# The second scoring of a tile's last 64 columns reads Q's high part from the first transposed block

## The chip, the cores and the metric

The kernel runs on one core of a Trainium2 chip. The metric is device time in microseconds (us), the median of the runs shown. Engines are named as the profile names them: PE is TensorE (PEld its weight loads), DVE is VectorE, ACT is ScalarE, POOL is GpSimd, SP is the queue that issues most DMAs.

## The reference

Attention over 8 batches x 8 heads, 576 rows of 64 numbers each, where every row keeps only its 32 largest scores; its output goes through a mixture of 8 experts, each of which takes 576 rows.

```
scores = q @ k.T / 8
kth = 32nd largest score of each row
scores = where(scores >= kth, scores, -1e9)
attn = softmax(scores);  x = attn @ v          # [4608, 512]
logits = x @ w_gate                            # greedy: the largest logits first, 576 rows an expert
out[rows of e] = relu(x[rows of e] @ w1[e]) @ w2[e]
```

## The kernel before, in words

**Pairs and tiles.** Attention goes over 32 pairs of heads, the experts follow. A pair has 9 tiles of 128 query rows (tiles 0 to 3 of one head, 5 to 8 of the other, tile 4 the last 64 rows of both, in two halves of 64 partitions).

**High and low parts.** Q and K are scaled and split into a high and a low f16 part, and turned by transposing DMAs (L394, for the first pair L395). Q's turned tile Qt has two blocks. The first, Q1, holds Q's high part on partitions 0 to 63 and its low part on 64 to 127. The second, Q2, holds the high part again on partitions 0 to 63, and on partition 64 a number per query row, 0 at first. K2 holds K's high part twice, K3 K's low part on partitions 0 to 63 and a constant on partition 64. KZ (two buffers, L251 to L252 and L396) holds K's low part of the last 128 columns on partitions 0 to 63, and zeros on 64 to 127.

**The work of a tile** (`tile_ops`, L429). PE scores it (L444 to L449): Q1 with K2 plus Q2 with K3, 512 columns ("s0") and the last 64 ("s1"). DVE takes the 8 largest of each of six chunks of 96 columns (L453, L454) and from these 48 the 24 largest in order (L457 to L461). ACT marks the scores above the 24th (`sign`, L466). PE then pushes the marked scores far down: `move(1)` for 512 columns ("o0", L471), `move(0)` for the last 64 ("o1"), which scores these 64 columns a second time (L470: Q1 with K2 plus Q2 with KZ), then adds the marks (L471) and eight more columns (L472). DVE finds the next 8 (`next8`, L473), so the 32nd is known; ACT makes a second mask from it (`relu`, L479). The scores stand in four PSUM lanes; a lane is free after L479.

**The row maxima.** As soon as the largest scores of three tiles (a trio) are known, POOL puts them beside Q's high part (`most`, L500), and one transposing DMA on SP writes these three tiles of Q2 anew, now with the maxima on partition 64 (`q2`, L501; three a pair, 96 in all, one for each trio). Q2 is thus written twice for a tile: by L394, and by L501.

**Softmax and values.** For each tile PE makes the turned masks (L515) and the scores turned (L520 with Q1, L521 with rows 0 to 64 of Q2, so with the maxima subtracted); ACT takes the exponential (L525), POOL splits it into two f16 parts (L528, L531), PE multiplies by V (L622), ACT scales (L596).

**What sets the order.** Every engine's order of work is fixed when the program is built: each step has a due time from a table (TAU, L268, period 24.5 us a pair) and a planner (`Loom`, L144) merges them. The planner's edges know that L501 needs the maxima and that the masks of a trio come after it; they hold nothing between L501 and `move(0)`. The semaphores come afterwards from the tile framework: it looks at what each instruction reads and writes, in the order of the plan. Where L501 stands in the plan between two `move(0)` of its trio, it waits for the reads of Q2 before it, and the reads of Q2 after it wait for its landing. SP's queue is in order; it also carries the loads of Q, K and V and L394.

Of the kernel before, what the change touches and what calls it, by code (L numbers as in the profile page):

```python
# [210 lines left out]
def attention(tc, q,k,v,w_gate,x_out,L,acc,cuts, pairs,ahead=()):  # L211
# [3 lines left out]
    with ExitStack() as ctx:  # L215
# [9 lines left out]
        def part(slot,kind,x,e):  # L225

            j,a=slot%(LANES//2),slot//(LANES//2)
            tc.add_to_no_dep_group(f"{j}{a}{kind}{e}",x.ins)
            for g in {"o":(f"{j}{1-a}o",f"{j}{1-a}m",f"{j}{1-a}t",f"{j}{a}t"),"t":(f"{j}{1-a}o",f"{j}{a}o"),"m":(f"{j}{1-a}o",)}[kind]:
                for o in "VAP":  # L230
                    if o!=e: tc.declare_no_dep(x.ins,group=g+o,reason="another bank")
            return x
# [15 lines left out]
        for i in range(2):  # L248
            t=cp.tile([128,2,9,128],F16,name=f"nq{i}"); NQ.append(t); V.memset(t[:,1,:,64:128],0.0)
            t=cp.tile([128,2,9,128],F16,name=f"nk{i}"); NK.append(t); V.memset(t[:,1,:,65:128],0.0); V.memset(t[:,1,:,64:65],-QS)  # L250
        KZ=[cp.tile([128,128],F16,name=f"kz{i}") for i in range(2)]  # L251
# [6 lines left out]
        def rims():  # L258
# [19 lines left out]
            k0=[15.592283,19.276599,21.411347,23.340401,28.448154,29.061625,31.74815,36.460414,37.611696],   # L278
# [150 lines left out]
        def tile_ops(P,i):  # L429
# [5 lines left out]
            def at_(): return D["at"]["slot"]  # L435
            def side(): return at_()//(LANES//2)
            def span(a,b):

                s_ps=SS[at_()%(LANES//2)]; o=960*side()
                return s_ps[:,o+a:o+b]  # L440
# [4 lines left out]
            def products(Q,K,n_,o,k0,kind,first,last):  # L445
                for h in ([0] if i<4 else ([1] if i>4 else [0,1])):
                    if i==4: rows=slice(h*64,h*64+64); qc=slice(512+h*64,576+h*64)
                    else: rows=slice(0,128); qc=slice(i*128,i*128+128)
                    part(at_(),kind,T.matmul(o[rows],P[Q][:n_,qc],P[K][:n_,k0(h):k0(h)+o.shape[1]],start=first,stop=last,skip_group_check=True),"P")  # L449
# [17 lines left out]
            def move(half):  # L467
                u=side(); o=64*u if half else 512*(1-u); n_=512 if half else 64
                if not half:
                    for Q,K,k0 in (("Q1","K2",512),("Q2","KZ",0)): products(Q,K,128,span(o,o+64),lambda h: k0+64*h,"t",Q=="Q1",False)  # L470
                part(at_(),"o" if half else "t",T.matmul(span(o,o+n_),off,P["w"][i][:,o:o+n_],start=False,stop=bool(half),skip_group_check=True),"P")  # L471
                if not half: part(at_(),"t",T.matmul(span(-8,0) if u else span(576,584),off,D["fw"][:,0:2,0:4],start=False,stop=True,skip_group_check=True),"P")  # L472
            def next8(): part(at_(),"m",V.max(P["st"][:,i,24:32],span(-8,576) if side() else span(0,584)),"V")  # L473
# [15 lines left out]
            p=tw=go("sg",sign,[p],take="w",e="A",d=0.717); mid.append(p)  # L489
            f_=go("fl",fill,[p],e="V",d=.11)  # L490
            p=go("o0",lambda: move(1),[p],e="P",d=.218)
            p=go("o1",lambda: move(0),[p,f_,P["kz"]],e="P",d=.125 if i==4 else .093,m=i==4); mid.append(p)
            p=go("y8",next8,[p],e="V",d=0.69); mid.append(p)
            p=go("rl",relu,[p],take="r",free=[ts],e="A",d=.63); P["tr"][i]=[p,tw]; mid.append(p)
# [925 lines left out]
```

## Time and profile before

| what | value |
|---|---|
| median of 3 runs | 1504.88 us (1500.55 to 1507.64) |
| profiled execution | 1496.38 us |
| its span, first to last instruction | 1494.7 us |
| attention, from the profile's lines | about 15 to 1040 us |
| mean granted clock of PE | 0.945 of 2.4 GHz |

The profile's page shows one execution: busy time of each engine, then groups of instructions with what they waited for. "Idle before" is the time the engine stood still ahead of an instruction, with the instruction or DMA that ended the wait. Matmuls overlap, and the shown length of one is longer than the distance to the next, so a busy PE is not PE at its peak. Granted clock is a share of 2.4 GHz: 0.50 means 1.2 GHz.

### The profile page before, as it was taken

The numbers are of one execution on the slowest core, as the hardware profiler recorded it, in microseconds if no ns is written. First come the engines' busy times: TensorE is split into PE (matmuls) and PEld (weight loads), VectorE is DVE, ScalarE is ACT, GpSimd is POOL, SyncE is SP. The second block draws the span as 40 slices with busy tenths as digits, with TensorE's granted clock in tenths as the row PEclk, the third lists the DMA queues.
The fourth block names the chain that finished last, engine by engine and source line by source line (L and its number), as shares of the span: only waits on it lengthen the run. The fifth ranks groups of instructions, "written<-read, shape, count | busy, mean of one in ns | idle before, by whom it ended". The sixth has DMA issues, their size and how long they took to land. (4 is left out here: it accounts for less than half of the span.)

```text
span 1494.7 us, 45618 instructions
## 1 busy us (share of the span) xinstructions
PE 1280.0 (86%) x17276; PEld 954.3 (64%) x17277; DVE 1102.4 (74%) x5557; ACT 934.4 (63%) x2177; POOL 822.2 (55%) x1090
## 2 busy tenths in 40 slices
PE   7778887888887888887888787888698999999998
PEld 5666666666666666666666665667674666566654
DVE  7777787877867777786777777786698999885410
ACT  3777777877867777786777777786133444325411
POOL 3776777767767776776676776775112312221011
PEclk9999999999989999998899999899699999999999
DMA  5443354334335343444433434330246666667001
GB/s 110 81 80 69 68 113 91 74 73 102 77 62 130 65 84 66 99 88 84 98 66 83 100 74 89 84 83 11 96 140 173 178 198 201 205 182 213 26 33 34
DMA packets 313130, 148.97 MB, mean 100 GB/s; under 512 B 278532, under 2 KB 294916, under 8 KB 311876
## 3 DMA queue, kind: packets, MB, share of 16 engines
q1 hardware_dynamic: 306530, 126.53, 36.1%
q0 software_dynamic: 5968, 19.14, 4.1%
q8 instruction: 137, 2.24, 0.6%
q14 instruction: 93, 0.76, 0.2%
q10 hardware_dynamic: 402, 0.29, 0.1%
HBM read 71.60 MB, written 18.87 MB: 61 GB/s over the span
## 5 line engine op out<-in xcount | busy, mean ns | idle before, releaser
L453 DVE MAX8 cd<-s 128x8 f32<-128x96 f32 x1440 | 318.2, 250 | 23.5 <-PE s L449 22.8
L449 PEld LDWEIGHTS <-Qt 128*128 128x128 f16 (+1 forms) x1920 | 149.7, 105 | 264.6 <-DMA Qt<-nq 189.2
L473 DVE MAX8 st<-s 128x8 f32<-128x584 f32 x288 | 216.8, 762 | 117.3 <-PE s L472 100.8
L449 PE MATMUL s<-Kt,Qt 128*128 128x64 f16 (+3 forms) x1600 | 289.5, 282 | 11.2 <-ACT w L466 8.1
L479 ACT ACTIVATE r<-s,st 128x576 bf16<-128x576 f32 x288 | 210.5, 739 | 130.9 <-DVE st L473 120.2
L531 POOL TENSOR_TENSOR elm<-F,ehm 128x512 f16<-128x512 f32 x253 | 287.8, 1159 | 0.2
L466 ACT ACTIVATE w<-s,st 128x576 uint16<-128x576 f32 x288 | 214.1, 743 | 60.9 <-PE s L472 50.8
L528 POOL TENSOR_SCALAR ehm<-F 128x512 f16<-128x512 f32 x253 | 154.4, 619 | 144.6 <-ACT F L525 144.3
L449 PE MATMUL s<-kz,Qt 128*128 128x64 f16 (+1 forms) x320 | 58.2, 206 | 169.3 <-DMA Qt<-nq 169.3
L1269 PE MATMUL ph<-xT,w1h 128*128 128x288 f16 (+1 forms) x1024 | 190.3, 286 | 3.6 <-DMA xT<-xs 3.6
L521 PE MATMUL pt<-Qt,Kt 65*128 65x128 f16 (+1 forms) x1280 | 179.4, 219 | 0.3 <-DMA Qt<-nq 0.3
L520 PE MATMUL pt<-Qt,Kt 128*128 128x128 f16 (+1 forms) x1280 | 179.2, 218 | 0.0
L525 ACT ACTIVATE F<-pt 128x512 f32<-128x512 f32 x256 | 148.8, 594 | 43.4 <-PE pt L521 39.9
L1329 POOL DMA_INDIRECT out_dram<-ob,idx x39 | 42.1, 1079 | 239.0 <-ACT ob L1324 222.4
L471 PE MATMUL s<-w,off 128*128 128x512 f16 (+1 forms) x576 | 154.0, 299 | 0.3 <-ACT w L466 0.2
L1269 PE MATMUL ph<-xT,w1l 128*128 128x288 f16 (+1 forms) x512 | 146.1, 286 | 0.0
L454 DVE MAX8 cd<-s 128x8 f32<-128x96 f32 x288 | 73.3, 255 | 90.0 <-PE s L449 58.2
L622 PE MATMUL pv<-vh,ehm 128*128 128x65 f16 x1012 | 124.2, 199 | 1.4 <-DVE xb L640 0.4
L622 PE MATMUL pv<-vh,elm 128*128 128x65 f16 x1012 | 124.4, 198 | 0.0
L622 PE MATMUL pv<-vl,ehm 128*128 128x65 f16 x1012 | 124.4, 198 | 0.0
L520 PEld LDWEIGHTS <-Kt 128*128 128x128 f16 x1280 | 120.7, 101 | 4.4 <-issue 0.7
L521 PEld LDWEIGHTS <-Kt 65*128 65x128 f16 x1280 | 120.5, 100 | 4.1 <-issue 0.3
(314 smaller groups left out, 3635.3 us busy)
## 6 DMA issues: line engine op xcount, KB each, us to landing
wr<-in_moe_w_dram SPq DMA_DIRECT2D x32, 1024.0 KB
kn<-in_k_dram SPq DMA_DIRECT2D x32, 256.0 KB
vt<-in_v_dram SPq DMA_DIRECT2D x64, 128.0 KB
x<-xb SPq DMA_DIRECT2D x8, 1024.0 KB
qn<-in_q_dram SPq DMA_DIRECT2D x31, 256.0 KB
Qt<-nq SPq DMA_TRANSPOSE x129
kn<-in_k_dram SPq DMA_DIRECT2D x32, 32.0 KB
vt<-in_v_dram SPq DMA_DIRECT2D x64, 16.0 KB
```

Source lines behind the costliest of these rows:

```text
L449: part(at_(),kind,T.matmul(o[rows],P[Q][:n_,qc],P[K][:n_,k0(h):k0(h)+o.shape[1]],start=first,stop=last,skip_group_check=True),"P")
L453: if c<5: part(at_(),"o",V.max(o,main(512-CW-CW*c,512-CW*c) if u else main(CW*c,CW*c+CW)),"V")
L466: part(at_(),"m",A.activation(D["w"],span(0,576),AF.Sign,bias=P["st"][:,i,32:33],scale=(1+2.0**-21),accum_out=acc[:,col]),"A")
L471: part(at_(),"o" if half else "t",T.matmul(span(o,o+n_),off,P["w"][i][:,o:o+n_],start=False,stop=bool(half),skip_group_check=True),"P")
L473: def next8(): part(at_(),"m",V.max(P["st"][:,i,24:32],span(-8,576) if side() else span(0,584)),"V")
L479: part(at_(),"m",A.activation(r,span(0,576),AF.Relu,bias=P["st"][:,i,31:32],scale=-1.0),"A")
L520: T.matmul(o,K2[:,kb:kb+128],Q1[:,qc],start=False,stop=False,skip_group_check=True)
L521: T.matmul(o,K3[0:65,kb:kb+128],Q2[0:65,qc],start=False,stop=(c==3 and h==sub[-1][0]),skip_group_check=True)
L528: G.tensor_scalar(D["eh"],D["E"],1.0,0.0,op0=ALU.mult,op1=ALU.add)
L531: G.tensor_tensor(el,D["E"],D["eh"],op=ALU.subtract); P["e"][i]=(D["eh"],el)
L622: for m_ in (range(N-3) if part==0 else range(N-3,N)): T.matmul(out,seq[m_][0],seq[m_][1],start=(m_==0),stop=(m_==N-1))
L1269: P.matmul(B["ph"][:,lo-c0:hi-c0],a[:,c,fs],xT[:,b+c,lo:hi],start=(i==0),stop=(i==11),skip_group_check=True)
```

## The change

The second product of the second scoring reads Q1 in place of Q2. Partitions 64 to 127 of KZ are zero, so the low part of Q in Q1 meets zeros, as partition 64 of Q2 did. The mark of the first product (it starts the sum) is taken from K's name, since Q's name is now the same for both. Nothing else is changed.

```
             def move(half):
                 u=side(); o=64*u if half else 512*(1-u); n_=512 if half else 64
                 if not half:
-                    for Q,K,k0 in (("Q1","K2",512),("Q2","KZ",0)): products(Q,K,128,span(o,o+64),lambda h: k0+64*h,"t",Q=="Q1",False)
+                    for Q,K,k0 in (("Q1","K2",512),("Q1","KZ",0)): products(Q,K,128,span(o,o+64),lambda h: k0+64*h,"t",K=="K2",False)
                 part(at_(),"o" if half else "t",T.matmul(span(o,o+n_),off,P["w"][i][:,o:o+n_],start=False,stop=bool(half),skip_group_check=True),"P")
```

## Rows read from the trace of the kernel before

**Rows 1.** Windows: us, busy time (instructions) of each engine, granted clock, DMA share, GB/s

```profile
100.00:1035.00 935.00, 772.55 (x12586) 608.47 (x12587) 717.08 (x4173) 707.60 (x1744) 670.56 (x902) 0.93 0.38 82
1035.00:1495.00 460.00, 433.07 (x3510) 285.47 (x3508) 311.55 (x933) 165.61 (x292) 94.07 (x92) 0.96 0.45 137
```

**Rows 2.** The page's groups: busy, mean ns of one, idle before and releaser

```profile
L449 PEld LDWEIGHTS <-Qt 128*128 128x128 f16 (+1 forms) x1920 | 149.7, 105 | 264.6 <-DMA Qt<-nq 189.2
L449 PE MATMUL s<-Kt,Qt 128*128 128x64 f16 (+3 forms) x1600 | 289.5, 282 | 11.2 <-ACT w L466 8.1
L449 PE MATMUL s<-kz,Qt 128*128 128x64 f16 (+1 forms) x320 | 58.2, 206 | 169.3 <-DMA Qt<-nq 169.3
```

**Rows 3.** Instructions on the tile kz: one copy a pair, first and last start

```profile
L396 POOL TENSOR_SCALAR kz<-Kt x32: 287/292/294, 15.1 to 996.3; 64x128 f16<-64x128 f16 x32
```

**Rows 4.** Line L501: its transposes, and who waited for them (us, times)

```profile
L501 SPq DMA_TRANSPOSE Qt<-nq x96: 1179/1229/2637, 26.6 to 1029.9; - x96
...
  PE s L449: 169.3, 94
  PE pt L521: 0.3, 1
```

**Rows 5.** Waits of other engines: us in total, times, longest

```profile
ACT r L479 <- DVE st L473: 120.2, 65, 4.0
DVE st L473 <- PE s L472: 100.8, 38, 4.2
DVE cd L454 <- PE s L449: 58.2, 31, 2.8
DVE cd L454 <- PE s L472: 30.0, 40, 3.2
```

**Rows 6.** Waits of the SP queue

```profile
SPq L501 <- PE s L472: 210.8, 32, 9.2
SPq L394 <- PE pt4r L574: 108.4, 30, 4.8
SPq L501 <- PE s L449: 34.2, 19, 8.7
```

**Rows 7.** Timeline around tile 4 of a pair: start, length, instruction, [idle before]

```profile
510.15 0.22 POOL L500 TENSOR_SCALAR nq<-st 128x3 f16<-128x3 f32 x1
510.95 1.22 SPq L501 DMA_TRANSPOSE Qt<-nq  x1
511.40 0.22 PE L449 MATMUL s<-Kt,Qt 128*64 128x64 f16 x2
514.92 0.13 PEld L449 LDWEIGHTS <-Qt 128*64 128x64 f16 x2 [3.41 <-DMA Qt<-nq]
514.92 0.27 PE L449 MATMUL s<-kz,Qt 128*64 128x64 f16 x2 [3.30 <-DMA Qt<-nq]
515.42 0.78 DVE L473 MAX8 st<-s 128x8 f32<-128x584 f32 x1 [3.62 <-PE s L472]
...
521.38 0.22 PE L521 MATMUL pt<-Qt,Kt 65*128 65x128 f16 x1
```

**Rows 8.** Windows: before, in and after such waits (columns as in rows 1)

```profile
507.00:511.00 4.00, 3.98 (x81) 3.47 (x80) 4.00 (x30) 3.92 (x10) 4.00 (x5) 1.00 0.80 155
...
513.00:515.00 2.00, 0.08 (x2) 0.08 (x2) 0.00 (x0) 0.00 (x0) 0.44 (x1) 0.64 0.49 94
515.00:521.00 6.00, 6.00 (x70) 4.56 (x71) 3.68 (x17) 2.69 (x8) 3.74 (x7) 0.55 0.38 71
535.00:545.00 10.00, 9.58 (x200) 7.62 (x197) 9.58 (x56) 9.92 (x24) 8.04 (x10) 1.00 0.48 59
```

**Rows 9.** Timeline around the last trio's transpose in the same pair

```profile
522.43 0.20 POOL L500 TENSOR_SCALAR nq<-st 128x3 f16<-128x3 f32 x1 [0.25 <-DVE st L457]
...
524.51 0.17 PE L472 MATMUL s<-fw,off 128*128 128x8 bf16 x1
...
524.70 1.18 SPq L501 DMA_TRANSPOSE Qt<-nq  x1
...
527.11 0.20 PE L449 MATMUL s<-kz,Qt 128*128 128x64 f16 x1 [0.82 <-DMA Qt<-nq]
...
529.14 0.22 PE L521 MATMUL pt<-Qt,Kt 65*128 65x128 f16 x1
```

More of the change, by code (lines that the diff above doesn't have):

```diff
@@ L469, in move @@
                 if not half:
-                    for Q,K,k0 in (("Q1","K2",512),("Q2","KZ",0)): products(Q,K,128,span(o,o+64),lambda h: k0+64*h,"t",Q=="Q1",False)
+                    for Q,K,k0 in (("Q1","K2",512),("Q1","KZ",0)): products(Q,K,128,span(o,o+64),lambda h: k0+64*h,"t",K=="K2",False)
                 part(at_(),"o" if half else "t",T.matmul(span(o,o+n_),off,P["w"][i][:,o:o+n_],start=False,stop=bool(half),skip_group_check=True),"P")
```

## The prediction, made before the changed kernel ran

> **What bounds the kernel now.** First the windows [rows 1]: attention is the longer stage, and in it PE, DVE, ACT and POOL are busy 83, 77, 76 and 72% of the time. No engine is full, so something makes them stand together. How long a pair takes comes from the one copy into KZ per pair [rows 3]: (996.3 - 15.1) / 31 = 31.65 us. Per pair PE is then busy 26.15 us, DVE 24.27, ACT 23.95 (share of the stretch times 31.65).
>
> Next the groups [rows 2]. PE stood 169.3 us ahead of the second product of the second scoring (`kz,Qt`), all of it put down to a DMA into Qt, while ahead of the first product and the other scorings it stood 11.2 us. Line L501 names the DMA [rows 4]: of its 96 transposes 94 were waited for at L449, 1.80 us each, three a pair; the softmax reader L521 waited once, 0.3 us. So PE's 5.5 idle us of a pair are nearly all these waits. The others wait in turn [rows 5]: ACT's second mask for DVE's `next8`, `next8` for the last matmul of the second scoring, DVE's sixth chunk for PE.
>
> The timeline shows one case [rows 7]. SP issues the trio's transpose at 510.95; PE runs the first product (Q1) at 511.40 without waiting for it, and stops at the load of the second one's weights until 514.92. That load reads Qt alone, and DVE stands 3.62 us behind it. The product does not need what the DMA brings: it wants the high part, which is the same before and after, and the maxima meet KZ's zeros.
>
> **The change, part by part.**
>
> *The instructions.* 320 weight loads and 320 matmuls read another block of the same tile in the same shape: 0 us. No instruction, DMA or planned step is added or moved, since the planner's edges did not know Q2 here.
>
> *The wait.* The read of Q1 doesn't overlap L501's write; that the tracking tells the blocks apart is shown by the first product, which ran while the transpose was on its way [rows 7]. Off PE's queue go 94 waits: -169.3 us [rows 4]. Queued behind the waiting matmul were the rest of PE's program, and `next8` and the mask on the other engines [rows 5].
>
> *The other side of the same edge.* L501 itself waited 210.8 + 34.2 us for matmuls of the second scoring (L472 comes right after the read) [rows 6]. Around the last trio [rows 9] POOL had the maxima at 522.63, but the transpose left at 524.70, behind the L472 of 524.51. It would now leave about 2.0 us earlier, and behind it on SP the loads of the coming pairs. I give that no time of its own: what reads them is covered by PE's work between. If that cover went, it would count for less than the wait removed.
>
> *Who is late next.* L521 still needs each transpose. Around tile 4 [rows 7] the landing is at 514.92 and, by the due times, the trio's first L521 at 521.38: 6.5 us for a PE that comes 3.3 us earlier. Around the last trio [rows 9] it is 2.0 us from 527.11 to 529.14, for a PE that comes 0.8 us earlier and a DMA that leaves 2.0 us earlier. The third transpose of a pair is read after the end of the former pair's softmax. I take 0 for new waits here; the bounds are 0 and, if every trio waited half as long as now, 85 us (94 x 0.9). L394, which writes Q1, is held until the corner's matmul L574 [rows 6], far behind any second scoring, so the new read of Q1 holds it no longer than before.
>
> *The clock.* Before the wait at tile 4 [rows 7, 8] the granted clock was 1.00; it was 0.64 around the wait's end and 0.55 in the six us after, so mostly the 1.2 GHz level, with PE busy throughout; in a later stretch without a wait it was 1.00 [rows 8]. Over 100 to 1035 us the mean of 0.93 means 2 x 0.07 x 935 = 131 us at 1.2 GHz, in which 65 us of full-speed work were lost [rows 1]. This can come back between 0 and 65 us. I take half, -33, since shorter gaps stay.
> The Trainium skill, "TensorE: Matmul & The Clock Gate", section "HAM oscillation — how this bites in real kernels", says that a wait in each step of a loop that is long enough throttles the array again, so every step begins cold; the windows agree, with 0.55 behind a 3.3 us wait [rows 8]. By it alone all 65 us would return.
>
> *What the other engines give back.* With -169.3 and -33 spread over 31 pairs a period would be 31.65 - 6.53 = 25.1 us. In the dense stretch DVE, PE and ACT are busy 96, 96 and 99% [rows 8]; DVE's 24.27 us at 96% are 25.3 us a pair. If DVE did nothing in today's waits (169.3 / 32 = 5.3 us a pair), it is 92% busy outside them: 24.27 / 0.92 = 26.4 us. I take the middle, 25.85 us. Against 25.1 that gives back (25.85 - 25.1) x 31 = 23 us; by the two ends 6 and 40.
>
> The experts' stage, 460 us [rows 1], has none of these products: 0.
>
> **Sum.** -169.3 - 33 + 23 = -179 us. Against the profiled execution's own 1496.4 us that makes 1317; that execution stands 8.5 us under the median of the runs, 1504.9, so I forecast 1504.9 - 179, about 1325 us. By the two ends of the period (25.3 and 26.4) 1308 to 1342.
>
> **The rivals.**
> *A: the wait moves to L521.* When PE runs ahead, each trio's transpose may be late for softmax instead, as POOL hands over the maxima in its own order, between long subtractions. For it: the 2.0 us of room around the last trio are little [rows 9]. Against it: one wait of 0.3 us at L521 today [rows 4], and SP freed earlier. With the 85 us bound, and the clock then partly low: 1325 + 85 = about 1410.
>
> *B: slower, by the clock.* Freed from one long wait, PE would meet DVE and ACT in many short ones, and its clock could sink to 1.2 GHz for most of attention. PE's work of a pair at full clock is 26.15 us less the 2.2 lost (65 / 935 x 31.65), 23.95 us. At a mean granted clock of 0.70 it would take 34.2 us, +2.6 x 31 = +79: 1584. It decides from 23.95 / 31.65 = 0.76 downward. For it: today PE also stands 11.2 us in short waits at its other scorings [rows 2]. Against it: in the dense stretch the clock was 1.00, and it fell behind the long waits [rows 8].
> The Trainium skill, same page, section "A second HAM failure mode: psum-queue depth-cycling", tells of such a kernel, whose clock swung because of small idle times between groups of matmuls. No run here shows it yet.
>
> *C: the change doesn't do what it says.* A wait for several semaphores is put down to the last; if the true releaser were another buffer's, the matmul would stand as before: about 1505. Against it: the weight load stood as long as the matmul (3.41 and 3.30 us), and it has no other tile to wait for [rows 7].
>
> **How the numbers follow.** Forecast 0.80, A 0.13, C 0.04, B 0.03. A measurement of this kernel can tell about 0.5% (8 us) from no change. Forecast and A are faster by more, C is the same, B slower: 0.93, 0.04, 0.03. The range: below, the waits and the whole clock gain and a DVE without any gap, 24.27 us a pair, would give 1504.9 - 31 x 7.38 = 1276; I stop a little above, at 1285. Above, it goes to 1400, which holds the forecast's own end (1342) and A with up to 75 of its 85 us. Left out are C, B, the far ends of A and of the low side, under 2 in 10.
>
> **What would show it.** Right: no idle time ahead of the `kz,Qt` group, L501 no longer waiting for L472, KZ copies 25.3 to 26.4 us apart, granted clock in attention above 0.96, DVE and ACT over 90% busy there, and experts of 460 us. Each step fails by its own row: waits at L521 (A), a low clock with many short idle times (B), the same wait at `kz,Qt` under another name (C), DVE under 90% busy with the waits gone (the amount given back is too small). The prediction is wrong if the period stays above 28.3 us, which would be 1400.

## The result, and the profile of the changed kernel

The changed kernel takes 1331.78 us (median of 4 runs, 1326.84 to 1334.34) beside 1506.26 us of the kernel before: a ratio of 0.8843, 95% interval 0.8806 to 0.8879. That is 174.5 us less; 179 were forecast. The order of instructions on every engine is the same in both kernels.

The busy rows of the page and the groups at L449 and L521 (columns as in [rows 2]):

```profile
PE 1241.3 (93%) x17276; PEld 932.6 (70%) x17277; DVE 1093.9 (82%) x5557; ACT 928.8 (70%) x2177; POOL 816.0 (61%) x1090
...
L449 PE MATMUL s<-Kt,Qt 128*128 128x64 f16 (+3 forms) x1600 | 281.9, 276 | 49.6 <-DMA Qt<-nq 47.8
...
L449 PEld LDWEIGHTS <-Qt 128*128 128x128 f16 (+1 forms) x1920 | 142.2, 103 | 121.9 <-DMA Qt<-nq 52.7
...
L521 PE MATMUL pt<-Qt,Kt 65*128 65x128 f16 (+1 forms) x1280 | 175.7, 216 | 4.7 <-DMA Qt<-nq 4.3
```

The `kz,Qt` group is no longer among the costly ones. The view of the tile kz has only the waits for Kt left ahead of its instructions, and gives the length of a pair by [rows 3]'s line. Line L501's view then shows the one reader that still waited for it:

```profile
L449 PE MATMUL s<-kz,Qt x320: 190/193/242, 21.9 to 872.2; 128*128 128x64 f16 x128, 128*64 128x64 f16 x32
L396 POOL TENSOR_SCALAR kz<-Kt x32: 288/291/293, 15.2 to 837.4; 64x128 f16<-64x128 f16 x32
...
  DMA Kt<-nk: 9.7, 3
...
  PE pt L521: 4.3, 6
```

A pair takes (837.4 - 15.2) / 31 = 26.52 us in place of 31.65. The windows of attention and of the experts, to be read beside [rows 1]:

```profile
100.00:870.00 770.00, 720.91 (x12395) 577.44 (x12396) 698.02 (x4117) 690.98 (x1715) 651.36 (x885) 0.97 0.47 99
870.00:1330.00 460.00, 434.61 (x3555) 286.29 (x3552) 312.98 (x939) 167.77 (x298) 97.83 (x95) 0.97 0.45 137
```

DVE is 91% busy and the granted clock rose from 0.93 to 0.97. From the start of the last second scoring to the end of the span it is 458 us (1330.2 - 872.2). Before it was 460 (1494.7 - 1034.6), by this line of the same view:

```profile
L449 PE MATMUL s<-kz,Qt x320: 190/193/263, 22.0 to 1034.6; 128*128 128x64 f16 x128, 128*64 128x64 f16 x32
```

So what follows the second scorings, nearly all of it the experts, takes the same within 2 us.

**The account on PE.** The spans differ by 1494.7 - 1330.2 = 164.5 us (less than the 174.5 of the medians, as the profiled execution of before lies 9.9 us under its median). PE's busy time fell from 1280.0 to 1241.3, so by 38.7 with the same 17276 matmuls; the rest, 125.8, is idle time. The 169.3 us ahead of `kz,Qt` are gone from it. Ahead of the other scorings the waits for Qt rose from 1.9 us (171.2 - 169.3, one wait) to 47.8 (31 waits), and at L521 from 0.3 to 4.3. That makes 169.3 - 45.9 - 4.0 = 119.4. Most of the other 6.4 us are the waits for ACT's marks, 8.1 us in [rows 2] and now 0.3. All waits of PE at the scorings for Qt before, then the waits for the marks after:

```profile
PE s L449 <- DMA Qt<-nq: 171.2, 95, 3.9
...
PE s L449 <- ACT w L466: 0.3, 2, 0.2
```

**The new wait** is one per pair, ahead of the next pair's first scoring. Line L394's view names its DMA:

```profile
L394 SPq DMA_TRANSPOSE Qt<-nq x31: 2385/2897/3928, 36.1 to 837.2; - x31
...
  PE s L449: 45.5, 30
```

The timeline of one pair, first POOL, then SP, then PE:

```profile
456.50 3.39 POOL L531 TENSOR_TENSOR elm<-F,ehm 128x512 f16<-128x512 f32 x3
459.86 0.20 POOL L500 TENSOR_SCALAR nq<-st 128x3 f16<-128x3 f32 x1
460.02 1.28 POOL L384 TENSOR_TENSOR nq<-scq,nq 128x576 f16<-128x576 f32 x1
...
460.03 0.59 SPq L364 DMA_DIRECT2D kn<-in_k_dram  x1
460.67 0.59 SPq L365 DMA_DIRECT2D kn<-in_k_dram  x1
461.72 1.22 SPq L501 DMA_TRANSPOSE Qt<-nq  x1
463.04 3.67 SPq L394 DMA_TRANSPOSE Qt<-nq  x1
...
468.78 1.04 PE L449 MATMUL s<-Kt,Qt 128*128 128x512 f16 x2 [2.76 <-DMA Qt<-nq]
```

The next pair's low part of Q is done at 461.3 (460.02 + 1.28), but its transpose leaves at 463.04, behind a load of K and the second trio's maxima. Here that is 1.7 us; over the 31 pairs the median is 1.0. In the kernel before the same transpose left right behind the one for which PE stood in [rows 7], and by L394's view only POOL's copies ever waited for a transpose of that line:

```profile
512.27 3.18 SPq L394 DMA_TRANSPOSE Qt<-nq  x1
...
  POOL kz L396: 2.2, 2
```

There it travelled while PE stood until 514.92, and its lateness, the same 1.0 us in the median, shows in no row of PE.

**On SP** the other side of the edge went as well. The queue's waits, to be read beside [rows 6]:

```profile
SPq L394 <- POOL elm L531: 152.1, 28, 7.2
SPq L501 <- POOL ehm L528: 123.2, 29, 5.2
...
SPq L394 <- PE pt4r L574: 50.8, 23, 2.5
SPq L501 <- PE s L449: 25.7, 13, 5.4
```

L501 waits for POOL now, which hands over the maxima, and not for L472. These rows count all the time in which the queue stood idle, though, also that in which the maxima were not there yet. How long L501 was held beyond the maxima can be worked out from the traces: from the end of each L500 to the start of its L501. For the 32 third trios this was 29.1 us in all before and is 0.8 now. For the first trios it was 2.1 and is 2.0, for the second ones 27.2 and 28.2. So what went with the change is some 28 us of holding (29.1 - 0.8), not the 245 of [rows 6].

### The profile page after: what moved, and what is told of

It is laid out like the page before. It is cut to its first block, busy times and chain, and to the rows that moved or that the text cites. A ratio compares the mean times of both kernels' runs of the same rounds, so it can differ in the third digit from the quotient of the medians.

```text
span 1330.2 us, 45619 instructions
## 1 busy us (share of the span) xinstructions
PE 1241.3 (93%) x17276; PEld 932.6 (70%) x17277; DVE 1093.9 (82%) x5557; ACT 928.8 (70%) x2177; POOL 816.0 (61%) x1090
## 5 line engine op out<-in xcount | busy, mean ns | idle before, releaser
L453 DVE MAX8 cd<-s 128x8 f32<-128x96 f32 x1440 | 315.4, 248 | 57.5 <-PE s L449 52.2
L449 PE MATMUL s<-Kt,Qt 128*128 128x64 f16 (+3 forms) x1600 | 281.9, 276 | 49.6 <-DMA Qt<-nq 47.8
L531 POOL TENSOR_TENSOR elm<-F,ehm 128x512 f16<-128x512 f32 x253 | 287.0, 1153 | 0.2
L449 PEld LDWEIGHTS <-Qt 128*128 128x128 f16 (+1 forms) x1920 | 142.2, 103 | 121.9 <-DMA Qt<-nq 52.7
L521 PE MATMUL pt<-Qt,Kt 65*128 65x128 f16 (+1 forms) x1280 | 175.7, 216 | 4.7 <-DMA Qt<-nq 4.3
L471 PE MATMUL s<-w,off 128*128 128x512 f16 (+1 forms) x576 | 148.5, 295 | 0.3 <-ACT w L466 0.2
L521 PEld LDWEIGHTS <-Kt 65*128 65x128 f16 x1280 | 118.8, 99 | 5.0 <-issue 1.9
L622 PE MATMUL pv<-vh,ehm 128*128 128x65 f16 x1012 | 118.1, 195 | 1.4 <-DVE xb L640 0.4
L622 PE MATMUL pv<-vl,ehm 128*128 128x65 f16 x1012 | 118.2, 193 | 0.0
L622 PE MATMUL pv<-vh,elm 128*128 128x65 f16 x1012 | 118.0, 193 | 0.0
L515 PE MATMUL pt<-out__184,r 128*128 128x128 bf16 (+1 forms) x1280 | 114.2, 217 | 1.0 <-ACT F L525 0.5
L515 PE MATMUL pt<-keep,w 128*128 128x128 bf16 (+1 forms) x1280 | 114.3, 217 | 0.0
```

The source lines that it names most:

```text
L453: if c<5: part(at_(),"o",V.max(o,main(512-CW-CW*c,512-CW*c) if u else main(CW*c,CW*c+CW)),"V")
L515: T.matmul(D["pt"][:,c*128+oc.start:c*128+oc.stop],mt[:,m0:m0+128],by[:,oc],start=first,**kw); first=False
L521: T.matmul(o,K3[0:65,kb:kb+128],Q2[0:65,qc],start=False,stop=(c==3 and h==sub[-1][0]),skip_group_check=True)
L531: G.tensor_tensor(el,D["E"],D["eh"],op=ALU.subtract); P["e"][i]=(D["eh"],el)
L622: for m_ in (range(N-3) if part==0 else range(N-3,N)): T.matmul(out,seq[m_][0],seq[m_][1],start=(m_==0),stop=(m_==N-1))
```

## Experiments

**Which side of the edge: PE's wait for L501, or L501's wait for PE?** The edge is the order that the framework keeps between L501, which writes Q2, and a second scoring that reads it; whichever comes later in the plan waits. L501 stands behind 83 of the 288 second scorings and ahead of 205. Two kernels keep one side each: raw_only lets PE wait (a read after a write), war_only lets L501 wait (a write after a read). In this fence and the next ones lines are cut to the parts that differ, with the run's name behind them; `sent`, empty at the start of a pair, collects the trios whose L501 has been issued.

```
-  (("Q1","K2",512),("Q1","KZ",0))
+  (("Q1","K2",512),("Q2" if i//3 in P["sent"] else "Q1","KZ",0))     # raw_only
+  (("Q1","K2",512),("Q1" if i//3 in P["sent"] else "Q2","KZ",0))     # war_only
-  def q2(): nc.sync.dma_start_transpose(
+  def q2(): P["sent"].add(i0//3); nc.sync.dma_start_transpose(           # both
```

raw_only: 

> Q2 is read in the second scoring only where L501 of the trio stands before it in the program (205 of 288 tiles); where L501 comes later Q1 is read, so L501 waits for no second scoring. Theory (PE's wait for the landing is the price): nearly all of the wait stays at the kz product, less what an L501 that leaves up to 2 us earlier takes from the third trio's waits (0.8 us each, about 30 of them): 1475 to 1506 us, and 130 to 170 us of idle time ahead of the kz product. Rival (the gain came from SP, freed of its 245 us of waits for the second scoring): close to the changed kernel, 1330 to 1360 us.

war_only: 

> The opposite: Q2 is read only where L501 of the trio comes later in the program (83 of 288 tiles), so L501 still waits for those matmuls, and no second scoring waits for L501. Theory: 0 us of idle time ahead of the kz product for L501, L501 waiting for L472 as before, and the time of the changed kernel within 1%, 1325 to 1345 us. Rival (SP freed): close to the kernel before, 1470 to 1506 us.

Measured: raw_only 1491.08 us, ratio 0.9863 (0.9817 to 0.9908); war_only 1337.08 us, ratio 0.8841 (0.8801 to 0.8881). The view of L501 in raw_only, who waited for it:

```profile
  PEld L449: 169.5, 81
  PE s L449: 155.2, 80
  PE pt L521: 0.4, 1
```

and the only waiter for L501 in war_only, with a row of its SP queue:

```profile
  PE pt L521: 7.2, 11
...
SPq L501 <- PE s L471: 56.9, 13, 5.7
```

Both times lie in the ranges of the theory. With 155.2 of the 169.3 us of waiting kept, nearly the whole time is kept; with PE free of L501, the whole gain is there. The third trios' transposes (from L500's end, as above) were held 0.9 us in all in raw_only, so L501 was free there as in the changed kernel, and 10.3 in war_only, so a third of the 29.1 was left, less than that theory said. The price was PE's wait for the landing; freeing SP by itself is not what paid.

**One trio or the others.** Two kernels make the change for a part of the tiles only.

```
+  ("Q1" if i//3==1 else "Q2","KZ",0)     # mid_trio
+  ("Q2" if i//3==1 else "Q1","KZ",0)     # outer_trios
```

mid_trio: 

> Q1 only in tiles 3 to 5 (the second trio); the other six tiles read Q2 as before. In the trace of before tile 4 held 86 us of the waits (30 of them, 2.9 us each) and the other tiles 83 us (64, 1.3 us each). Theory (the clock's loss hangs on the long waits alone): this run gets 86 us of waits and most of the clock's gain (44 us of lost work), less up to 20 us for whatever is late next: 1376 to 1400 us, granted clock in attention at 0.96 or above. Rival (the clock's loss belongs to all waits alike): 86 and about 22 us, 1398 to 1420 us, clock about 0.95.

outer_trios: 

> Q1 in tiles 0 to 2 and 6 to 8; tiles 3 to 5 read Q2 as before. Theory (clock loss hangs on the long waits of tile 4): only the 83 us of short waits go, the clock stays at about 0.93: 1415 to 1435 us. Rival (clock loss belongs to all waits alike): 83 and about 22 us, 1395 to 1412 us. If the two halves add up, the gains of this run and of the run with tiles 3 to 5 alone come to the 174 us of the whole change.

Measured: mid_trio 1457.90 us, 0.9655 (0.9612 to 0.9697), slower than theory and rival allowed; outer_trios 1401.43 us, 0.9275 (0.9239 to 0.9311), faster than the theory and inside the rival's range. The gains, 52 and 109 us, add to 161 of the 174.

mid_trio's waits on PE at L449, first the part that is L501's, then L394's, then all:

```profile
  PE s L449: 86.6, 59
...
  PE s L449: 38.4, 30
...
PE s L449 <- DMA Qt<-nq: 126.5, 90, 3.4
```

Of the 83 us that went with tiles 3 to 5, 38.4 came back as waits for the other DMA into Qt, L394. In outer_trios, where tile 4 still waits, PE never waited for L394; all waits but L501's are 95.6 - 93.5 = 2 us there:

```profile
  PE s L449: 93.5, 31
...
PE s L449 <- DMA Qt<-nq: 95.6, 32, 4.0
```

So the wait at tile 4 covered L394, and taking it away lets the wait for L394 appear. The attention windows of mid_trio and then of outer_trios:

```profile
100.00:995.00 895.00, 770.80 (x12573) 610.57 (x12571) 714.30 (x4167) 707.05 (x1746) 669.90 (x902) 0.93 0.42 86
...
100.00:941.00 841.00, 748.21 (x12607) 598.14 (x12605) 708.27 (x4162) 704.82 (x1743) 666.68 (x897) 0.95 0.42 91
```

The theory of the clock failed: with the long waits of tile 4 kept and the short ones gone, the clock was 0.95 and PE's busy time some 24 us lower than in [rows 1]. The other run says less: without tile 4's waits for L501 the clock stayed at 0.93 and the busy time at that of [rows 1], but other waits grew, up to 3.4 us. The loss was not that of the long waits alone.

**Is the wait for L394 what the change did not gain, or would DVE have taken it?** Each of these kernels is the changed one with due times moved: `tq` is that of L394's transpose of Q, `lq` that of Q's low part on POOL, `ldk` that of the load of K. The counts of filler matmuls are held at those of the changed kernel.

```
-  lq=[15.156738]   tq=[-1.341912]   ldk=[-29.010665]
+                   tq=[-1.7]                           # tq_early
+  lq=[9.5]         tq=[-1.7]                           # both_early
+  lq=[9.5]         tq=[-1.7]        ldk=[-32.1]        # all_early
```

after_again: 

> The changed kernel itself, as the measure for the other three on the same chip: 1325 to 1345 us by every theory, with about 48 us of PE's time lost ahead of the scorings that read the next pair's Q (L394).

tq_early: 

> The changed kernel with one due time moved, so that on SP the next pair's Q (L394) goes ahead of the second trio's transpose (L501) instead of behind it; the filler matmuls are held as they are. L394 leaves about 1.3 us earlier (one L501 issue of 1.22 us), the trio's maxima come some 3 us later. Theory (what the kernel did not gain is the wait for L394, 48 us, 1.5 us a pair): most of this wait goes, 1290 to 1318 us, unless L521 now waits for the trio (then L521's wait shows it). Rival (DVE, busy 91% in attention, sets the pace and would take up what PE gains): 1322 to 1340 us.

both_early: 

> As the run before, and on POOL the next pair's low part of Q goes ahead of three long subtractions and the second trio's maxima. L394 can then leave about 4 us earlier than in the changed kernel. Theory: the whole wait for L394 goes, 48 us, 1284 to 1305 us, DVE 94% busy or more in attention. Rival (DVE sets the pace): 1322 to 1340 us; a softmax that gets its second trio late would show as waits at L521 and eat some 10 us.

all_early: 

> As the run before, and the load of a coming pair's K goes on SP ahead of the turned K instead of between it and the turned Q, so that 1.2 us more are taken from in front of L394, and POOL's scaling of K, which waits 80 us in all for this load, finds it there. Theory (L394 is enough): the same as the run before within 0.5%. Rival (the K load and POOL's wait are part of the loop): 10 to 25 us faster than the run before.

Measured: 1336.99 for the changed kernel again, then 1371.63, 1387.29 and 1387.91 us. The first two are slower than theory and rival said; all_early equals both_early, as its theory had it. The wait for L394 did go, but each put something later that was wanted just as soon. Waits of PE in tq_early (the second trio's maxima), then of PE and POOL in both_early between 100 and 850 us (the subtractions that POOL now makes after Q's low part):

```profile
PE pt L521 <- DMA Qt<-nq: 71.4, 32, 3.3
PE s L449 <- DMA Qt<-nq: 4.3, 2, 2.2
```

```profile
PE pv L622 <- POOL elm L531: 76.3, 26, 2.9
...
POOL nq L384 <- ACT nq L378: 64.6, 26, 2.8
```

In both_early POOL reached Q's low part (L384) before ACT had the high part (L378) and stood 64.6 us in all, and the three subtractions (L531) behind it came late. all_early, with the load of K also moved, shows the same 76.3 us at L622; that POOL's order set the pace in both is the likely reading. These three couldn't tell the theories apart, as each took a new wait for the old one. What was wanted was an edit that puts nothing back.

```
-  ldk=[-29.010665]
+  ldk=[-32.1]                                          # kn_early
```

after_beside: 

> The changed kernel once more, as the measure for the next run on the same chip: 1325 to 1345 us by every theory.

kn_early: 

> The changed kernel with one due time moved: on SP the load of a coming pair's K goes ahead of the turned K, where SP waits for POOL in any case, instead of ahead of the second trio's transpose and the turned Q; the filler matmuls are held as they are, and nothing on POOL, ACT, DVE or PE changes its order. L501 and L394 can both leave about 1.2 to 1.6 us earlier. Theory (the 48 us wait for L394 is lost time, and the two runs before lost because what they put back, the second trio's maxima or POOL's subtractions, is needed just as soon): the wait falls to 15 us or less with no new one, 1290 to 1312 us. Rival (DVE, 91% busy, sets the pace and takes up what PE gains): the wait falls likewise, but the time stays within 1% of the run beside it, 1322 to 1340 us.

Measured, side by side: 1330.79 us (0.8804, 0.8769 to 0.8839) and 1283.85 us (0.8497, 0.8469 to 0.8526). The waits for Qt and one window of attention in after_beside, then the same in kn_early with its copies into KZ, which give the pair:

```profile
PE s L449 <- DMA Qt<-nq: 44.6, 30, 2.9
...
100.00:800.00 700.00, 654.03 (x11233) 522.86 (x11232) 633.37 (x3733) 629.25 (x1556) 596.85 (x811) 0.97 0.49 101
...
PE s L449 <- DMA Qt<-nq: 18.5, 20, 2.1
...
L396 POOL TENSOR_SCALAR kz<-Kt x32: 287/291/304, 15.5 to 788.3; 64x128 f16<-64x128 f16 x32
...
100.00:800.00 700.00, 676.95 (x11947) 544.63 (x11945) 669.16 (x3958) 665.50 (x1655) 635.83 (x862) 1.00 0.51 108
```

The wait fell from 44.6 us in the run beside it to 18.5, a little above the 15 expected, and the time fell by 47 us, somewhat more than expected; a pair takes 24.93 us. DVE rose from 90 to 96% busy and PE from 93 to 97%, with the clock at 1.00. So DVE did not set the pace of the changed kernel: there were 47 us between it and this version, which is the fastest of the study, 223.7 us under the kernel before it ran beside.

L394's transpose now leaves 0.06 us after Q's low part is done (median of 31), where the run beside it has 1.06. Between the two profiles PE's waits for Qt fell by 26.1 us at the scorings and by 5.7 at L521 (6.4 to 0.7), and its busy time by 18.4 (1238.6 to 1220.2): together 50.2, about what the span lost (1329.8 to 1281.5). But the edit took away one thing more, POOL's wait for the load of K, in after_beside and then in kn_early:

```profile
POOL sck L383 <- DMA kn<-in_k_dram: 81.7, 30, 5.6
...
POOL sck L383 <- DMA kn<-in_k_dram: 3.0, 1, 3.0
```

No run takes that wait away alone, so what it adds to the 47 us is not shown.

## Why the prediction held, and where it did not

*The wait.* Forecast -169.3; measured, all of the L501 waits ahead of `kz,Qt` are gone. raw_only and war_only show that this wait, and not L501's own, carried the time. The reading that did it was the pair in [rows 7]: the product that reads Q1 ran, and the weight load that reads only Q2 stood.

*The other side of the edge.* Given no time; war_only, which keeps a third of it, is within 0.5% of the changed kernel, and raw_only, which takes it away, is only 19 us under the kernel before, with 14 us less of PE's wait for L501. Right. The 2.0 us of [rows 9] were more than the usual case: the mean of the third trios was 0.9 (29.1 / 32).

*The clock.* Forecast -33 between 0 and -65; PE's busy time fell by 38.7. The size was right. Between 100 and 870 us the clock was still 0.97. In outer_trios, with one long wait a pair, it was 0.95, and in mid_trio, without tile 4's, 0.93, so the loss cannot be laid on one long wait per pair alone. In kn_early, where hardly a wait is left, it was 1.00. By the passage of "TensorE: Matmul & The Clock Gate" (the Trainium skill, section "HAM oscillation — how this bites in real kernels") alone, as the prediction took it, all 65 would have come back. The changed kernel does not bear that out; kn_early, with the next wait mostly gone too, comes close to it.

*Who is late next.* Here the prediction failed: "I take 0 for new waits". It looked at L521, the next reader of what L501 brings, and was right on it (4.3 us). It looked at L394 only as a writer that might be held up longer. It didn't ask who waits for L394's landing, though SP sends it right behind the trio for which tile 4 stood. That wait measured 45.5 us by L394's view.

*What the other engines give back.* Forecast +23, by DVE's share, between 6 and 40. The account gives 169.3 + 38.7 - 164.5 = 43.5 us given back, above that range, and its cause is not DVE but the new waits, L394's above all: no wait of PE for DVE or ACT grew by more than 2 us, and kn_early ran DVE at 96%, as the dense stretch of [rows 8] had it. A wrong reason thus stood in for the missing wait, and that the sum came near (1325 forecast, 1331.8 measured; a pair 25.85 and 26.52 us) was in part luck: the middle between 92% and 96% happened to leave room for it. The 96% end, 25.3 us a pair, is near what the machine did (24.93) once the order let it.

*The rivals.* A: 4.3 us at L521, not 85. B: the clock rose. C: the wait did not stay under another name. None came true, though tq_early shows A's mechanism at work when the order favours it: 71.4 us at L521.

*The signs.* Two of those named for a right forecast were just missed: a pair of 26.52 us where 25.3 to 26.4 was said, and ACT 89.7% busy (690.98 of 770) where it was over 90%.

## What to carry to other kernels

A read of a buffer that is written again can cost the wait for the landing even where the value wanted is the same in both versions (1.80 us each here); look for another copy of the value before looking for a faster transfer. Before pricing a removed wait at its whole length, list every transfer that was in flight during it, with its reader: here the one next in the queue was the next wait. And where an in-order queue has a slot in which it stands anyway, move into that slot the work that stands ahead of something urgent, as kn_early did; a swap of two urgent things only moved the wait here.

## What the runs showed that was not expected

The share of half-speed clock did not follow tile 4's long waits: mid_trio without them 0.93, outer_trios with them 0.95. Why was not settled.

One transposing DMA (L501) took 510.95 to 514.92, 3.97 us, from its issue until PE ran, where L394's transpose of Q left 1.32 us behind it, and another of the same size 2.41 us (524.70 to 527.11) with plain loads behind it [rows 7, 9]. Over the kernel before, the median is 3.4 us for the 31 second trios with L394 behind them and 2.4 us for the 29 third trios with loads behind them. That the second transpose stretches the first fits. But the last pair has no L394 behind its second trio and took 3.8 us there, so L394 cannot be the only reason; no run took it away alone, and it stays open.
